# A quarter of one weight load cut into 88 and 40 rows, and four unread matmuls taken out, in a one-token decoder block

## The chip, the cores and the metric

The kernel runs on one core of a Trainium2 chip. Its time is the device time of one execution in microseconds (us), as the median of several runs. The profile is of one execution, recorded by the hardware profiler; its span reaches from the first to the last instruction of the program. PE is TensorE, PEld its weight loads, DVE is VectorE, ACT ScalarE, POOL GpSimd, and SP is SyncE, which here only issues loads and the one store.

## The reference

A decoder block for one new token of two sequences: layer norm, attention over a cache of 8,192 keys and values with 16 heads, a residual, a second layer norm, and a gated feed-forward part without a nonlinearity, with its residual.

```python
B, Sq, D = 2, 1, 448            # H, Sk, Dh = 16, 8192, 256;  F = 1792
q = (layernorm(x) @ wq).reshape(B, Sq, H, Dh).transpose(0, 2, 1, 3)
p = softmax(einsum("bhqd,bhkd->bhqk", q, k_cache) * Dh ** -0.5)
h = x + einsum("bhqk,bhkd->bhqd", p, v_cache).reshape(B, Sq, H * Dh) @ wo
g, u = layernorm(h) @ w_gate, layernorm(h) @ w_up
out = h + (g * u) @ w_down
```

All is float32. Each cache has 2 x 16 x 8,192 x 256 elements, 268 MB.

## The kernel before

**The turns.** There are 32 turns, one for each head of each sequence. For a turn SP loads the keys (128 rows of 64 x 256 elements, 8.4 MB) into one of two buffers, `k0` and `k1`, and the values, of the same size, into `v`. VectorE multiplies the keys by the query and sums each product (lines 436 and 445), TensorE and ScalarE make the exponentials, and TensorE sums the weighted values (line 527) in bank 0.

**The order of the loads.** SP issues all of them itself, in an order written out in lines 261 to 292, and they all go into one queue. A load waits until its buffer is free: keys for the maximum `m` of the turn two before, values for the end `M` of the sums of the turn before. Behind the last keys come `wo` into the free half of the key buffers, the last values in two pieces (48 and 16 of 64 columns), then `wg`, the gate weights, once the last keys are used, then `wu`, the up weights, in three loads, then, once the last values are used, `wd`, the down weights, in six loads. Each of the three up loads and six down loads has a semaphore of its own, so that a matmul can start when its own piece has landed. A load's semaphore counts 16 when all of it is there.

**The last stage**, after the 32 turns. TensorE multiplies the last head by `wo`; ScalarE takes the sum `h`; the norm's centred input is made as `xr` (line 676). Then `project` (line 710) runs twice: the gate, 12 matmuls by line 715 and two by line 726, from `wg`; and up, the same from `wu`. In up, the first 8 of line 715 wait for the first up load (contraction chunks 0 and 1), the next 4 for the second, and the two of line 726 for the third. ScalarE scales the gate (line 746), VectorE multiplies it by up (line 755), TensorE transposes the product (line 760), VectorE copies it (line 767), and TensorE multiplies it by the 14 pieces of `wd`: 8 of them by line 779, the others by line 805, each waiting for its wd load. VectorE copies the result (line 815), and SP stores it.

**Unread matmuls.** `busy(n)` (line 534) issues four matmuls of n columns into bank 4, which nobody reads any more. It is called at six places: before the last turn's transposes (384 columns), twice around `last_head` (256 and 320), between gate and up (384), after up (256) and before the down matmuls (192). They are the L539 of the profile.

**Layout of the up weights.** `wu` lies in memory as 128 rows of 6,272 elements. The first up load takes the first 2 F = 3,584 elements of each row, the second the next F = 1,792, the third the last 896.

Of the kernel before, what the change touches and what calls it, by code (L numbers as in the profile page):

```python
# [8 lines left out]
B, D, H, SK, DH, F = 2, 448, 16, 8192, 256, 1792  # L9
EPS = 1e-5  # L10
P = 128
# [13 lines left out]
NF = F // P  # L25
FH = FG[0] // 2
FF = [(n, g) for n in range(4) for g in range(4) if n < FG[g] // P]
DOWN = (4, 4, 2, 2, 1, 1)
NPART, OPEN_AFTER = 8, 9

LAYOUT = (
# [122 lines left out]
def decode_block(nc, x, k_cache, v_cache, wq, wo, wg, wu, wd, out):  # L154
# [6 lines left out]
    def landing(name):  # L161
        return nc.alloc_semaphore(name=name)
# [4 lines left out]
    V, A, G, S, T = (  # L167
        Engine(nc, *engine)
        for engine in (
            (nc.vector, "dve"), (nc.scalar, "act", ("qsel", "qb"), ("q",)), (nc.gpsimd, "pool"),  # L170
            (nc.sync, "sp"), (nc.tensor, "pe", ("qp", "Q0"), ("heads",)),
        )
    )

    def load(line, dst, src, sem, name, *waits, n=16):
        line.do(lambda: line.e.dma_start(dst, src).then_inc(sem, 16), *waits)  # L176
        known[name] = sem, n
# [63 lines left out]
    wu_t = k_flat[1][:, NF * D : 2 * NF * D]  # L241
# [39 lines left out]
        )  # L281
        at += n
    load(S, wg_t, wg, landing("wg"), "wg", ("m", NQ - 1))
    for k, part in enumerate((slice(0, 2 * F), slice(2 * F, 3 * F), slice(3 * F, NF * D))):
        load(S, wu_t[:, part], wu[:, part], landing(f"wu{k}"), ("wu", k))
    at = 0
    for k, n in enumerate(DOWN):
        load(
# [245 lines left out]
    def busy(n):  # L534


        for g in range(0, P, 32):
            T.do(
                lambda g=g: nc.tensor.matmul(  # L539
                    acc_ps[g : g + B, :n], sel, heads[:, :n], start=True, stop=True  # L540
                )
            )
# [130 lines left out]
    for rows, c, to in LAYOUT:  # L673
        k = rows.stop - rows.start
# [35 lines left out]
    def project(ps, w, landed, done, blank, between=None):  # L710

        for c in range(DC - 1):
            for g, n in enumerate(FG):
                T.do(
                    lambda c=c, g=g, n=n: nc.tensor.matmul(
                        ps[32 * g : 32 * g + 32, :n], xr[:, c].rearrange("p b r -> p (b r)"),
                        w[:, c * F + FO[g] : c * F + FO[g] + n], start=(c == 0), stop=False,
                    ),
                    landed(c), "xr", blank,
                )  # L720
            if c == 1 and between is not None:
                between()
        at = (DC - 1) * F
        for k in range(2):
            T.do(
                lambda k=k, n=FG[2 * k], at=at: nc.tensor.matmul(
                    ps[HALF * k : HALF * k + HALF, :n],
                    xr[:, DC - 1 :].rearrange("p c b r -> p (c b r)"), w[:, at : at + n],
                    start=False, stop=True,
                ),  # L730
                landed(DC - 1), done=done if k == 1 else None,
            )
            at += FG[2 * k]
# [11 lines left out]
    A.do(  # L745
        lambda: nc.scalar.activation(g_sb, g_ps, AF.Copy, scale=rv), "g", "rv", done="g_in",
    )
    busy(384)
    project(u_ps, wu_t, lambda c: ("wu", max(c - 1, 0)), "u", "u_blank")
    busy(256)  # L750
    hm_sb, hmT = late(P, FG[0]), late(P, 4, P)
# [23 lines left out]

    down_of = [k for k, n in enumerate(DOWN) for _ in range(n)]
    for k, (j, g) in enumerate(FF[:NPART]):
# [105 lines left out]
```

## Time and profile before

| | us |
|---|---|
| three runs: median (lowest, highest) | 1301.18 (1301.15, 1301.63) |
| the profiled execution | 1300.94 |
| its span | 1299.6 |
| DVE busy | 1132.5 (87%) |
| PE busy | 471.1 (36%) |
| SP's queue on the 16 DMA engines | 99.8% of the span |

The profiled execution is 0.24 us under the median of the runs, and 1.34 us of it lie outside the span. Busy shares are means over the whole span. In windows, the DMA share is the mean over 16 DMA engines, so that one engine at work alone shows as 0.06. A packet is put into the window in which it starts, so a share can pass 1.00.

### The profile page before, as it was taken

The numbers are of one execution on the slowest core, as the hardware profiler recorded it, in microseconds if no ns is written. First come the engines' busy times: TensorE is split into PE (matmuls) and PEld (weight loads), VectorE is DVE, ScalarE is ACT, GpSimd is POOL, SyncE is SP. The second block draws the span as 40 slices with busy tenths as digits, with TensorE's granted clock in tenths as the row PEclk, the third lists the DMA queues.
The fourth block names the chain that finished last, engine by engine and source line by source line (L and its number), as shares of the span: only waits on it lengthen the run. The fifth ranks groups of instructions, "written<-read, shape, count | busy, mean of one in ns | idle before, by whom it ended". The sixth has DMA issues, their size and how long they took to land.

```text
span 1299.6 us, 7381 instructions
## 1 busy us (share of the span) xinstructions
PE 471.1 (36%) x2870; PEld 149.9 (12%) x2870; DVE 1132.5 (87%) x265; ACT 83.5 (6%) x245; POOL 0.8 (0%) x8
## 2 busy tenths in 40 slices
PE   3643214334323433323334322433322343332368
PEld 0111001101001101101101101101100110100113
DVE  1999988889888889888889988889988888988861
ACT  1100000000000000000000000000000000000000
POOL 0000000000000000000000000000000000000000
PEclk9866566666566666556666656666656666655669
DMA  9999999999999999999999999999999999999998
GB/s 412 428 450 422 448 424 444 426 436 436 422 450 422 450 422 448 424 444 426 436 436 422 450 422 450 422 448 424 444 426 436 436 422 450 422 450 422 448 422 365
DMA packets 11382, 561.28 MB, mean 432 GB/s; under 512 B 1394, under 2 KB 1652, under 8 KB 2420
## 3 DMA queue, kind: packets, MB, share of 16 engines
q1 hardware_dynamic: 11376, 561.25, 99.8%
q8 instruction: 2, 0.03, 0.0%
q10 hardware_dynamic: 4, 0.00, 0.0%
HBM read 561.19 MB, written 0.06 MB: 432 GB/s over the span
## 4 chain that ended last, share of the span: by engine, by line
DMA 48%; DVE 41%; issue 8%; PE 2%; SPq 0%; DVEq 0%; ACT 0%
DMA k<-in_A_k_cache_dram 45%; DVE s L445 21%; DVE k L436 19%; DMA v<-in_wq_dram 2%; DMA v<-in_wd_dram 1%; PE bank L376 1%; PE bank L561 1%; PE bank L527 1%; DVE m L458 0%; DVE nm L464 0%; DVE rl L469 0%; SPq L176 0%; PE bank L551 0%; DVEq L149 0%; PE bank L367 0%
## 5 line engine op out<-in xcount | busy, mean ns | idle before, releaser
L436 DVE TENSOR_TENSOR k<-k,qb 128x4096 f32<-128x4096 f32 x64 | 555.3, 8676 | 122.6 <-DMA k<-in_A_k_cache_dram 98.9
L445 DVE TENSOR_REDUCE s<-k 128x16 f32<-128x4096 f32 x64 | 555.2, 8675 | 1.1
L527 PE MATMUL bank<-v,p 128*2 128x512 f32 x2048 | 289.5, 729 | 348.0 <-DMA v<-in_A_v_cache_dram 348.0
L527 PEld LDWEIGHTS bank<-v,p 128*2 128x2 f32 x2048 | 53.2, 96 | 577.2 <-DMA v<-in_A_v_cache_dram 370.7
L597 PE MATMUL bank<-nm,row 1*128 1x1 f32 x64 | 18.6, 357 | 230.9 <-DVE nm L464 230.9
L594 PE MATMUL bank<-ident,m 128*1 128x128 f32 x32 | 11.9, 372 | 179.7 <-DVE m L458 179.7
L502 ACT ACTIVATE o_sb<-bank 128x512 f32<-128x512 f32 x32 | 19.1, 597 | 625.9 <-PE bank L527 625.9
L597 PEld LDWEIGHTS bank<-nm,row 1*128 1x128 f32 x64 | 15.9, 306 | 240.3 <-DVE nm L464 240.3
L619 PE MATMUL bank<-sel,o_sb 128*128 128x1 f32 x256 | 33.7, 253 | 22.6 <-ACT o_sb L502 22.6
L367 PE MATMUL bank<-q_sel,ones 2*128 2x256 f32 x68 | 40.2, 691 | 0.0
L619 PEld LDWEIGHTS bank<-sel,o_sb 128*128 128x128 f32 x256 | 31.0, 191 | 52.3 <-ACT o_sb L502 52.3
L376 PE MATMUL bank<-v,xz 128*2 x64 | 30.5, 639 | 16.3 <-DMA v<-in_wq_dram 16.3
L492 ACT ACTIVATE nb<-bank 128x1 f32<-128x1 f32 x32 | 5.5, 171 | 427.0 <-PE bank L597 427.0
L601 PE MATMUL bank<-lsum,ones 128*128 128x1 f32 x64 | 18.7, 361 | 23.5 <-ACT p L494 23.5
L594 PEld LDWEIGHTS bank<-ident,m 128*1 128x1 f32 x32 | 2.5, 79 | 182.7 <-DVE m L458 182.7
L601 PEld LDWEIGHTS bank<-lsum,ones 128*128 128x128 f32 x64 | 16.0, 309 | 26.2 <-ACT p L494 26.2
L404 ACT ACTIVATE q_sel<-q_all,ident 2x256 f32 (+1 forms) x35 | 17.2, 492 | 0.0
L413 ACT ACTIVATE qb<-bank 128x256 f32<-128x256 f32 x34 | 13.0, 383 | 58.2 <-PE bank L367 58.2
L367 PEld LDWEIGHTS bank<-q_sel,ones 2*128 2x128 f32 x68 | 16.4, 297 | 2.2 <-issue 1.7
L494 ACT ACTIVATE p<-s,nb 128x64 f32<-128x64 f32 x32 | 11.1, 348 | 1.0
L504 ACT ACTIVATE oT<-bank,rl 128x2 f32 x32 | 8.4, 262 | 42.0 <-PE bank L619 42.0
L487 DVE COPY k<-bank 128x448 f32<-128x448 f32 x1 | 0.6, 624 | 11.6 <-PE bank L561 11.6
(89 smaller groups left out, 96.0 us busy)
## 6 DMA issues: line engine op xcount, KB each, us to landing
v<-in_wq_dram SPq DMA_DIRECT2D x1, 7168.0 KB, 19.7
k<-in_wo_dram SPq DMA_DIRECT2D x1, 7168.0 KB, 39.6
k<-in_A_k_cache_dram SPq DMA_DIRECT2D x1, 6144.0 KB, 38.1
v<-in_A_v_cache_dram SPq DMA_DIRECT2D x1, 6144.0 KB, 22.8
k<-in_wg_dram SPq DMA_DIRECT2D x1, 3136.0 KB, 27.8
k<-in_A_k_cache_dram SPq DMA_DIRECT2D x1, 2048.0 KB, 24.1
v<-in_A_v_cache_dram SPq DMA_DIRECT2D x1, 2048.0 KB, 27.3
k<-in_wu_dram SPq DMA_DIRECT2D x1, 1792.0 KB, 31.8
```

Of the source, the lines that this page charges most:

```text
L367: lambda *_: nc.tensor.matmul(qb_ps, ones[:B, :], q_sel, start=True, stop=True),
L376: lambda turn, k=k, c=c, xs=xs, base=base: nc.tensor.matmul(q_ps[k], xz[:, xs, :], wq_t[:, bass.ds(turn * QG + base, QG)], start=(c == 0), ...
L404: return nc.scalar.activation(q_sel, q_sb[:, bass.ds(at, DH)], AF.Copy, scale=ident[:B, b : b + 1])
L413: lambda *_: nc.scalar.activation(qb[i % 2], qb_ps, AF.Copy),
L436: lambda *_: nc.vector.tensor_mul(kt, kt, q[:, None, :].to_broadcast([P, hi - lo, DH])),
L445: lambda *_: nc.vector.tensor_reduce(s[:, lo:hi], kt, axis=AX.X, op=ALU.add),
L502: A.do(lambda *_: nc.scalar.activation(o_sb, o_ps, AF.Copy), ("M", i), done=("osb", i))
L527: lambda *_, t=t, g=g: nc.tensor.matmul(o_ps[g : g + 2, :], p_t[:, 2 * t : 2 * t + 2], v_sb[:, 2 * t : 2 * t + 2, :], start=(t < 4), stop= ...
L594: lambda *_: nc.tensor.transpose(mT_ps, m_t, ident), ("m", i), done=("T", i)
L597: lambda *_: nc.tensor.matmul(nb_ps, row, nm, start=True, stop=True),
L601: lambda *_: nc.tensor.matmul(l_ps, ones, lsum, start=True, stop=True),
L619: lambda *_, c=c, k=k: nc.tensor.matmul(oT_ps[:, c : c + 1], o_sb[:, (2 * k + c) * P : (2 * k + c + 1) * P], sel[:, k : k + 1], start=(k = ...
```

## The change

The first quarter of the first up load, F / 2 = 896 of its 3,584 elements of each row, is loaded on its own, in two loads: rows 0 to 87 and rows 88 to 127. The rest of the first up load, elements 896 to 3,583 of all rows, follows. All three count on the first up load's semaphore, and its readers wait for 48 in place of 16. The second and third up load are as they were. The four unread matmuls between gate and up are gone; nothing they wrote was read.

```diff
+EVEN = 88
...
-    for k, part in enumerate((slice(0, 2 * F), slice(2 * F, 3 * F), slice(3 * F, NF * D))):
-        load(S, wu_t[:, part], wu[:, part], landing(f"wu{k}"), ("wu", k))
+    wu_ends, s_wu = (2 * F, 3 * F, NF * D), [landing(f"wu{k}") for k in range(3)]
+    for rows in (slice(0, EVEN), slice(EVEN, P)):
+        load(S, wu_t[rows, : F // 2], wu[rows, : F // 2], s_wu[0], "wu_even")
+    for k, part in enumerate(map(slice, (F // 2, *wu_ends), wu_ends)):
+        load(S, wu_t[:, part], wu[:, part], s_wu[k], ("wu", k), n=16 * (3 if k == 0 else 1))
...
-    busy(384)
     project(u_ps, wu_t, lambda c: ("wu", max(c - 1, 0)), "u", "u_blank")
```

On SP, the loads from the gate weights on stood like this before (rows x elements of each load; k and v are the buffers, and waits names the semaphores: dve0 is VectorE's, pe0 TensorE's):

```order
L176 DMA k<-in_wg_dram 128x6272 [waits dve0]
L176 DMA k<-in_wu_dram 128x3584
L176 DMA k<-in_wu_dram 128x1792
L176 DMA k<-in_wu_dram 128x896
L176 DMA v<-in_wd_dram 128x1792 [waits pe0]
```

and stand so now (the line of the helper that issues is now 179):

```order
L179 DMA k<-in_wg_dram 128x6272 [waits dve0]
L179 DMA k<-in_wu_dram 88x896
L179 DMA k<-in_wu_dram 40x896
L179 DMA k<-in_wu_dram 128x2688
L179 DMA k<-in_wu_dram 128x1792
L179 DMA k<-in_wu_dram 128x896
L179 DMA v<-in_wd_dram 128x1792 [waits pe0]
```

SP issues two loads more ahead of the wd loads; nothing else changes place on it.

On TensorE, the end of gate and the start of up before (sel and xr are the left operands, wu0 and wu1 the semaphores of the first two up loads):

```order
L726 MATMUL bank<-k,xr 64x512
L726 MATMUL bank<-k,xr 64x384
L539 MATMUL bank<-k,sel 2x384 x4
L715 MATMUL bank<-k,xr 32x512 [waits dve0,wu0]
L715 MATMUL bank<-k,xr 32x512
L715 MATMUL bank<-k,xr 32x384 x2
```

and now:

```order
L732 MATMUL bank<-k,xr 64x512
L732 MATMUL bank<-k,xr 64x384
L721 MATMUL bank<-k,xr 32x512 [waits dve0,wu0]
L721 MATMUL bank<-k,xr 32x512
L721 MATMUL bank<-k,xr 32x384 x2
```

Up follows the gate's last matmul directly; it waits for the same semaphores.

## The prediction

> **What bounds the kernel now.** I read the page first, for shares and queues.
>
> ```profile
> PE 471.1 (36%) x2870; PEld 149.9 (12%) x2870; DVE 1132.5 (87%) x265; ACT 83.5 (6%) x245; POOL 0.8 (0%) x8
> ...
> DMA packets 11382, 561.28 MB, mean 432 GB/s; under 512 B 1394, under 2 KB 1652, under 8 KB 2420
> ...
> q1 hardware_dynamic: 11376, 561.25, 99.8%
> q8 instruction: 2, 0.03, 0.0%
> q10 hardware_dynamic: 4, 0.00, 0.0%
> ```
>
> Queue 1, which is SP's, keeps the 16 DMA engines busy for 99.8% of the span at a mean of 432 GB/s, or 432 / 16 = 27.0 GB/s for each. The two caches and the weights are 561 MB, and the change moves no byte less. VectorE's 87% lies in front of these transfers and isn't touched. So the end of the kernel is set by when the last bytes arrive, and only the last stage can give anything. Its chain of waits, from the issue of the last wd load on:
>
> ```profile
> 1279.27 0.04 issue
> 1279.31 17.89 DMA v<-in_wd_dram
> 1297.20 0.04 issue
> 1297.24 0.44 PE bank L805 x8
> 1297.69 0.02 issue
> 1297.71 0.27 DVE k L815
> ```
>
> The last wd load lands at 1297.20 us; only eight records of matmul, one copy and the store of the result come after it. A finer look is at the same stretch by windows; the columns are the window, its length, busy time (and count) of PE, PEld, DVE, ACT and POOL, the granted clock, the DMA share and GB/s.
>
> ```profile
> 1290.00:1291.00 1.00, 1.00 (x6) 0.20 (x4) 0.00 (x0) 0.00 (x0) 0.00 (x0) 1.00 1.01 423
> 1291.00:1292.00 1.00, 1.00 (x12) 0.31 (x10) 0.74 (x2) 0.00 (x0) 0.00 (x0) 1.00 1.00 419
> 1292.00:1293.00 1.00, 1.00 (x16) 0.48 (x18) 0.78 (x3) 0.00 (x0) 0.00 (x0) 1.00 1.00 409
> 1293.00:1294.00 1.00, 0.77 (x12) 0.07 (x8) 0.00 (x0) 0.00 (x0) 0.00 (x0) 1.00 1.01 412
> 1294.00:1295.00 1.00, 0.86 (x8) 0.04 (x8) 0.07 (x1) 0.00 (x0) 0.00 (x0) 1.00 1.01 396
> 1295.00:1295.60 0.60, 0.45 (x16) 0.38 (x16) 0.56 (x1) 0.00 (x0) 0.00 (x0) 1.00 0.85 326
> 1295.60:1296.00 0.40, 0.40 (x16) 0.16 (x8) 0.00 (x0) 0.00 (x0) 0.00 (x0) 1.00 0.22 81
> 1296.00:1296.90 0.90, 0.76 (x26) 0.51 (x24) 0.00 (x0) 0.00 (x0) 0.00 (x0) 1.00 0.13 48
> 1296.90:1298.80 1.90, 0.58 (x16) 0.16 (x8) 0.27 (x1) 0.00 (x0) 0.00 (x0) 1.00 0.00 0
> ```
>
> The sixteen DMA engines do not stop together. The share falls from 0.85 to 0.22 at about 1295.6 and to 0.13 after 1296.0: 0.22 x 16 = 3.5 engines, then 0.13 x 16 = 2.1. So about thirteen are done by 1295.6, one or two more by 1296.0, and two work on alone to 1296.9, 1.3 us behind the mass. The last landing waits for those two. The likely cause is in the queue rows: two packets of kind "instruction" took DMA time during the run. This is the row of the second, from the DMA view of 1282 to 1284 us:
>
> ```profile
> q8 instruction: 1, 0.02, 3.0%
> ```
>
> 3.0% of 16 engines' 2 us is 0.96 us of one engine. The view of 77 to 79 us shows the other. Each would put one engine behind by about the 1.3 us seen, and with the queue never empty it cannot catch up. That is a reading; no row numbers the engines.
>
> **The change part by part.** The split load first. Where were the up loads issued and when did they land?
>
> ```profile
> L176 SPq DMA_DIRECT2D k<-in_wu_dram x3: 419/433/433, 1254.6 to 1255.6; - x3
> ...
> k<-in_wu_dram SPq DMA_DIRECT2D x1, 1792.0 KB, 31.8
> k<-in_wu_dram SPq DMA_DIRECT2D x1, 896.0 KB, 33.4
> ...
> k<-in_wu_dram SPq DMA_DIRECT2D x1, 448.0 KB, 34.0
> ```
>
> *Issue.* Two more issues on SP at 0.43 us each are 0.87 us. Behind them on SP stand the six wd loads and the store. SP's next wait ends at 1276.97 (row below), the three issues end at 1255.6 + 0.4 = 1256.0, so 21 us of idle SP hide it, and the transfers themselves start some 25 us after their issue in any case. Cost 0; uncovered it would be 0.87 us.
>
> *Bytes.* The quarter is 128 rows of 3,584 B, 0.459 MB: 1.06 us at 432 GB/s, or 1.11 at the 412 GB/s of the window from 1293, where packets of this size run. Smaller packets thus cost at most 0.05 us on all engines.
>
> *Which engine moves what.* By count, SP issues 79 loads and stores of 128 rows each (4 ahead of the loop, 61 in it, 14 behind), and 79 x (128 + 16) = 11,376, exactly queue 1's packets: one packet for each row and one closing packet for each of 16 engines. The only short transfer is x:
>
> ```profile
> x<-in_A_x_dram ACTq DMA_DIRECT2D x1, 3.5 KB
> ```
>
> Its 2 rows gave queue 10's four packets, 2 + 2: two engines. Both fit a rule of equal shares, 8 rows on each of 16 engines and 1 row on each of 2. By equal shares 88 rows go to 11 engines (8 each) and 40 to 10 (4 each), the greatest divisors up to 16. If both start at the same end of the list, ten engines carry 12 rows of the quarter in place of 8, one carries 8, five none. A row takes 3,584 B / 27.0 GB/s = 0.133 us, so the ten finish 0.53 us later and the five 1.06 us earlier. The bounds from rows: if instead rows are spread as evenly as they go (5 or 6 and 2 or 3 to an engine), nothing moves by more than one row, 0.13 us.
>
> [...] No run here has yet shown which engines a load of 88 rows uses.
>
> *What that does to the end.* Before, the mass ends at 1295.6, the one or two between at 1296.0 and the two late ones at 1296.9.
>
> - Case A, both late engines among the five: they end at 1296.9 - 1.06 = 1295.84. The mass goes to 1295.6 + 0.53 = 1296.13, the one between to 1296.53 if it is among the ten. The last is then at 1296.13 to 1296.53: 0.37 to 0.77 us earlier. I take 0.37, since the engine between has 11 chances in 16 to be outside the five, and with it the packets' 0.05 us: -0.32 us.
> - Case B, one of the two among the ten: it ends at 1296.9 + 0.53 + 0.05, so +0.58 us.
>
> Even a perfect levelling, with the surplus of the late ones dealt out to all, gains no more than 1.3 - 2.1 x 1.3 / 16 = 1.1 us.
>
> *The removed matmuls.* From the timeline, with start, duration and engine:
>
> ```profile
> 1276.97 3.27 SPq L176 DMA_DIRECT2D v<-in_wd_dram  x6
> ...
> 1286.82 0.83 PE L539 MATMUL bank<-k,sel 128*2 128x384 f32 x8
> ...
> 1287.46 2.74 PE L715 MATMUL bank<-k,xr 128*32 128x512 f32 x24
> ...
> 1290.14 1.07 PE L726 MATMUL bank<-k,xr 128*64 128x512 f32 x4
> ...
> 1292.77 0.94 PE L779 MATMUL bank<-v,k 128*2 128x448 f32 x8
> 1293.93 0.11 PEld L779 LDWEIGHTS bank<-v,k 128*2 128x2 f32 x8 [1.05 <-DMA v<-in_wd_dram]
> 1293.93 0.93 PE L779 MATMUL bank<-v,k 128*2 128x448 f32 x8 [0.23 <-DMA v<-in_wd_dram]
> ...
> 1297.24 0.40 PE L805 MATMUL bank<-v,k 128*32 128x112 f32 x8 [0.16 <-DMA v<-in_wd_dram]
> ```
>
> Without L539 up can start at 1286.82 in place of 1287.46, 0.64 us earlier; its first load landed at 1254.63 + 31.8 = 1286.4. Its L726 then waits for the third up load, 1255.6 + 34.0 = 1289.6, in place of starting at 1290.14: about 0.5 us gained on PE. But PE then only waits longer for wd: at 1293.93 the second wd load holds it already, and it is the last wd load that holds it at 1297.24. So this edit gives 0 by itself. In case A it gives slack to a PE that would have only the 0.23 and 0.16 us of these two waits left; if PE's work were late, up to 0.2 us of A would be lost.
>
> *The wait on the first up load* now counts three transfers. It lands as a whole at 1286.4, or 0.53 later (1286.9) in the worst case, against PE's arrival at 1286.82: at most 0.1 us, which the 0.5 us freed covers.
>
> *The PE clock.* The removed work kept PE without a pause. What does a pause do? Two rows, of a pause before the last turn and of the end:
>
> ```profile
> 1249.00:1254.20 5.20, 0.00 (x0) 0.00 (x0) 5.17 (x2) 0.22 (x1) 0.00 (x0) 0.76 1.14 495
> ...
> 1295.00:1299.60 4.60, 2.19 (x56) 1.20 (x56) 0.83 (x2) 0.00 (x0) 0.00 (x0) 0.99 0.20 71
> ```
>
> In 5.2 us of idle the mean clock is 0.76, so it was full for 0.52 of it, 2.7 us, and half after. At the end, with PE busy for 2.19 of 4.6 us, it stayed at 0.99. The new pause is 0.5 us: cost 0. [...]
>
> **The sum.** The profiled execution took 1300.94 us, 1.34 over its span of 1299.6, and 0.24 under the median of three, 1301.18. Case A gives 1300.94 - 0.32 = 1300.62, that is 1300.86 against the median.
>
> **The rivals.** *B, one late engine carries more* (+0.58): 1301.76. For it: five places in sixteen are few, and drawn blindly both late engines are in them only in one case of twelve. Against it: an engine that fetches code need not be drawn at random, and two late engines need not be far apart. No row settles it, so choosing A over B is a judgment.
>
> *E, the change does not do what it says*: rows are spread evenly, or the engine of 8 rows is the late one. 0 to +0.05: 1301.2. For it: no row shows a load of 88 rows, so an even spread is not excluded. Against it: the equal shares in the counts of packets. [...]
>
> *C, the clock halves*, the side slower by more than 0.2%. If the pauses in up or ahead of wd reach some 2.7 us, PE's remaining groups (from L726 to L805, 6.8 us busy from 1290 on by the windows above) run at half the clock. The 3.8 us of them from 1293 on would take 3.8 us longer, all of them 6.8. Less the waits for wd that this swallows, about 1 us, it is 2.8 to 5.8: 1304.0 to 1307.0. Against it: the pause is a fifth of what the clock bore.
>
> **How the numbers follow.** About 0.2%, 2.6 us, is what a measurement of this kernel can tell from no change. A has 0.50, B 0.33, E 0.14, C 0.03. A, B and E all lie within 2.6 us; no mechanism above gains over 1.1, which leaves 0.01 for faster, and C gives 0.03 for slower. The forecast is A's 1300.9, no change that can be told. The range reaches from A's best, 0.77 us less (1300.4), to B's 1301.8 with 0.2 us for the runs' own spread: 1300.4 to 1302.0. C is left out.
>
> **What would show it.** Right: in the windows of the last 3 us, the share stays above 0.5 to about 1296.1 and then drops within 0.5 us; the last wd landing at 1296.9 or before; L726 of up starting at about 1289.6; the clock at 1.00. B: a thin tail of 0.06 to 0.13 for 2 us and more, the last landing near 1297.8. E: the windows as before. Wrong altogether: a clock of 0.5 before 1297, or a span that differs by over 2.6 us.

## The result, and the profile after

The changed kernel takes 1302.96 us (median of 22 runs, 1301.87 to 1305.43), against 1301.18 for the kernel before (22 runs, 1300.96 to 1301.73): a ratio of 1.0016, with a 95% interval of 1.001 to 1.0021. That is 1.8 us slower, less than the 0.2% (2.6 us) that the prediction took as the least that can be told, and yet clear: the fastest run of the changed kernel is slower than the slowest of the kernel before. It lies outside the predicted range of 1300.4 to 1302.0. One thing about the median has to be known: the 22 runs of the changed kernel lie in two groups, 12 of them from 1301.87 to 1303.11 (median 1302.09) and 10 from 1304.00 to 1305.43 (median 1304.61), with nothing between, while those of the kernel before lie in one group of 0.8 us. So there are two amounts to explain, 0.9 us that every run loses, and 2.5 us more in nearly half of them.

The profiled execution of the changed kernel took 1303.11 us, the highest of the lower group; its span is 1301.8. The queues on its page:

```profile
DMA packets 11531, 561.28 MB, mean 431 GB/s; under 512 B 1415, under 2 KB 1673, under 8 KB 2569
...
q1 hardware_dynamic: 11525, 561.25, 99.8%
q8 instruction: 2, 0.03, 0.0%
```

The bytes are the same, and queue 1 has 11,525 - 11,376 = 149 packets more: 128 rows and 21 closing packets. 21 is 11 + 10, so the 88 rows went to 11 engines and the 40 to 10, as the equal shares said.

The windows of the kernel before, in the microseconds in which the short loads will run (columns as in the prediction; the last two are DMA share and GB/s):

```profile
1281.00:1282.00 1.00, 1.00 (x11) 0.90 (x11) 0.02 (x1) 0.00 (x0) 0.00 (x0) 1.00 1.00 430
1282.00:1283.00 1.00, 1.00 (x8) 0.36 (x10) 0.89 (x6) 0.00 (x0) 0.00 (x0) 1.00 1.00 418
1283.00:1284.00 1.00, 1.00 (x15) 0.47 (x8) 0.68 (x4) 0.00 (x0) 0.00 (x0) 1.00 0.97 401
1284.00:1285.00 1.00, 1.00 (x12) 0.46 (x10) 0.06 (x1) 0.00 (x0) 0.00 (x0) 1.00 0.92 387
```

The same of the changed kernel, then its end:

```profile
1281.00:1282.00 1.00, 0.96 (x9) 0.58 (x7) 0.17 (x1) 0.35 (x2) 0.00 (x0) 1.00 1.05 297
1282.00:1283.00 1.00, 1.00 (x10) 0.69 (x10) 0.41 (x3) 0.00 (x0) 0.00 (x0) 1.00 1.06 233
1283.00:1284.00 1.00, 0.39 (x3) 0.00 (x0) 0.83 (x6) 0.00 (x0) 0.00 (x0) 1.00 1.07 215
1284.00:1285.00 1.00, 0.75 (x10) 0.43 (x14) 0.35 (x2) 0.00 (x0) 0.00 (x0) 1.00 0.96 317
1285.00:1286.00 1.00, 1.00 (x12) 0.17 (x4) 0.00 (x0) 0.00 (x0) 0.00 (x0) 1.00 1.08 437
...
1297.00:1297.60 0.60, 0.36 (x17) 0.34 (x16) 0.48 (x1) 0.00 (x0) 0.00 (x0) 1.00 0.86 329
1297.60:1298.20 0.60, 0.60 (x20) 0.20 (x11) 0.14 (x1) 0.00 (x0) 0.00 (x0) 1.00 0.60 227
1298.20:1299.10 0.90, 0.81 (x24) 0.51 (x24) 0.00 (x0) 0.00 (x0) 0.00 (x0) 1.00 0.06 22
```

From 1281 to 1285 the sixteen engines are as busy as ever, at shares of 0.96 to 1.07, and yet move 215 to 317 GB/s in place of 387 to 430. The share says here that packets were under way, not that they went at full rate: in the packet records of this trace a row of 3,584 bytes takes 140 ns elsewhere in this stage, and 259 ns in the median of those that start in the microsecond from 1282. At the end the shape that case A forecast is there, though 2 us late. The mean share is 0.60 until 1298.2, and then 0.06, one engine of sixteen, is alone for 0.9 us; before, two engines were alone, 1.3 us behind. In another execution of the changed kernel, after_look1 below, no engine is left alone for long:

```profile
1297.80:1298.40 0.60, 0.60 (x24) 0.23 (x12) 0.00 (x0) 0.00 (x0) 0.00 (x0) 1.00 0.20 75
1298.40:1299.00 0.60, 0.43 (x12) 0.16 (x8) 0.00 (x0) 0.00 (x0) 0.00 (x0) 1.00 0.00 0
```

The same stage of the changed kernel's profile in the timeline:

```profile
1255.23 2.08 SPq L179 DMA_DIRECT2D k<-in_wu_dram  x5
...
1284.25 1.91 PE L721 MATMUL bank<-k,xr 128*32 128x512 f32 x16 [0.86 <-DMA k<-in_wg_dram]
...
1288.64 1.91 PE L721 MATMUL bank<-k,xr 128*32 128x512 f32 x16 [0.18 <-DMA k<-in_wu_dram]
...
1290.78 1.05 PE L721 MATMUL bank<-k,xr 128*32 128x512 f32 x8 [0.23 <-DMA k<-in_wu_dram]
...
1291.85 1.07 PE L732 MATMUL bank<-k,xr 128*64 128x512 f32 x4
...
1296.12 0.93 PE L784 MATMUL bank<-v,k 128*2 128x448 f32 x8 [0.70 <-DMA v<-in_wd_dram]
...
1299.39 0.40 PE L810 MATMUL bank<-v,k 128*32 128x112 f32 x8 [0.16 <-DMA v<-in_wd_dram]
```

From the gate weights on, PE waits for a transfer ahead of nearly every group that reads a new load; before, its matmuls waited for none of this stage's loads until the wait for wd at 1293.93 (row in the prediction). The last matmuls start at 1299.39 in place of 1297.24, 2.15 us later. Of these, 0.6 us were there ahead of the short loads: the up loads are issued from 1255.23 on, in place of 1254.6. That is part of what makes this execution the slowest of its group. The other 1.5 us come in from the short loads on.

### The profile page after: what moved, and what is told of

It reads as the page before. It is cut to its first block, busy times and chain, and to the rows that moved or that the text cites. A ratio compares the mean times of both kernels' runs of the same rounds, so it can differ in the third digit from the quotient of the medians.

```text
span 1301.8 us, 7367 instructions
## 1 busy us (share of the span) xinstructions
PE 469.5 (36%) x2862; PEld 149.4 (11%) x2862; DVE 1132.6 (87%) x265; ACT 83.5 (6%) x245; POOL 0.8 (0%) x8
## 3 DMA queue, kind: packets, MB, share of 16 engines
q1 hardware_dynamic: 11525, 561.25, 99.8%
## 4 chain that ended last, share of the span: by engine, by line
DMA 75%; PE 25%; issue 0%; SPq 0%; DVE 0%
DMA v<-in_A_v_cache_dram 72%; PE bank L533 22%; PE bank L382 2%; DMA v<-in_wq_dram 2%; DMA v<-in_wd_dram 1%; SPq L179 0%; PE bank L373 0%; PE bank L810 0%; DVE k L820 0%
## 5 line engine op out<-in xcount | busy, mean ns | idle before, releaser
L508 ACT ACTIVATE o_sb<-bank 128x512 f32<-128x512 f32 x32 | 19.1, 597 | 628.0 <-PE bank L533 628.0
```

What stands on the lines that cost most here:

```text
L508: A.do(lambda *_: nc.scalar.activation(o_sb, o_ps, AF.Copy), ("M", i), done=("osb", i))
```

## The experiments

Theories of the 0.9 us: **T1**, rows that lie next to each other in a short load are contested: they hold one another up, by something that no view names, and so take about twice as long (259 ns in place of 140 in the profile after); the dip of the windows is theirs. **T2**, the shares of 11 and 10 engines are unequal, and an engine that had no slack has more to carry. **T2b**, short loads cost as such. **T3**, it is the removed matmuls. **T4**, it is smaller packets. Theories of the second group: **T5**, the clock halves; **T6**, a transfer comes later. Each kernel below starts from the kernel before; every time stands against the kernel before on the same chip.

**split_only, nobusy_only: the two parts of the change apart.** The first has the change's loads and keeps all unread matmuls; the second only leaves out the four:

```diff
-    busy(384)
     project(u_ps, wu_t, lambda c: ("wu", max(c - 1, 0)), "u", "u_blank")
```

> The kernel before with the split of the quarter into 88 and 40 rows alone; the four unread matmuls stay. [...] Theory 2 (unequal shares alone, a late engine given 12 rows for 8): +0.6 us and no dip. Theory 3 (the removed matmuls cost it, by a pause of PE): within 0.2 us of before.

> The kernel before without the four unread matmuls between gate and up; loads as before. Theories 1 and 2: within 0.2 us of before, since PE waits for the down weights at 1293.9 and 1297.2 us anyway. Theory 3: +1.3 to +2.5 us.

split_only: 1302.28 us (11 runs) against 1301.16, ratio 1.0015 [1.0005, 1.0024], with 4 of its 11 runs at 1304.42 to 1304.9. nobusy_only: 1301.53, 1.0002 [0.9993, 1.0011], in one group. That is 0.37 us above before, over the 0.2 that was expected, but inside the interval, and its runs (1300.97 to 1301.87) overlap with those of before (1300.82 to 1301.84). The split alone has both the loss and the second group. T3, which expected 1.3 us or more, falls; a few tenths are not excluded.

**halves64: equal shares, contested rows** (shown against split_only's loads, with EVEN = 88, as is the next).

```diff
-    for rows in (slice(0, EVEN), slice(EVEN, P)):
+    for rows in (slice(0, 64), slice(64, P)):
```

> The kernel before with the quarter as rows 0 to 63 and rows 64 to 127; the unread matmuls stay. Both loads give 4 rows to each of 16 engines, so shares are equal. [...] Theory 2: within 0.2 us of before, no dip.

**cols_only: the quarter as a load of its own, all 128 rows.**

```diff
-    for rows in (slice(0, EVEN), slice(EVEN, P)):
-        load(S, wu_t[rows, : F // 2], wu[rows, : F // 2], s_wu[0], "wu_even")
+    load(S, wu_t[:, : F // 2], wu[:, : F // 2], s_wu[0], "wu_even")
```

> The kernel before with the quarter (896 elements of each row) as a load of its own over all 128 rows; the unread matmuls stay. Theories 1 and 2: within 0.2 us of before (one issue more and smaller packets, 0.05 us). Theory 4 (smaller packets or one load more are what costs): +1 us or more.

halves64: 1302.98 (1302.55 to 1303.33), 1.0013 [1.0004, 1.0022], 1.8 us more, and one group. cols_only: 1301.25 (1301.13 to 1301.7), 1.0 [0.9991, 1.0009]. The windows of the same microseconds, of cols_only:

```profile
1281.00:1282.00 1.00, 1.00 (x11) 0.94 (x12) 0.00 (x0) 0.00 (x0) 0.00 (x0) 1.00 1.08 448
1282.00:1283.00 1.00, 1.00 (x8) 0.36 (x10) 0.88 (x6) 0.00 (x0) 0.00 (x0) 1.00 1.04 441
1283.00:1284.00 1.00, 1.00 (x15) 0.47 (x8) 0.71 (x4) 0.00 (x0) 0.00 (x0) 1.00 0.99 414
1284.00:1285.00 1.00, 1.00 (x12) 0.43 (x10) 0.03 (x1) 0.00 (x0) 0.00 (x0) 1.00 0.96 391
```

and of halves64, with its last microseconds:

```profile
1281.00:1282.00 1.00, 1.00 (x11) 0.93 (x12) 0.00 (x0) 0.00 (x0) 0.00 (x0) 1.00 1.35 294
1282.00:1283.00 1.00, 0.81 (x4) 0.17 (x2) 0.88 (x6) 0.00 (x0) 0.00 (x0) 1.00 0.68 204
...
1296.60:1297.20 0.60, 0.37 (x12) 0.17 (x12) 0.30 (x1) 0.00 (x0) 0.00 (x0) 1.00 0.41 155
1297.20:1297.80 0.60, 0.60 (x24) 0.36 (x18) 0.32 (x1) 0.00 (x0) 0.00 (x0) 1.00 0.12 48
1297.80:1298.40 0.60, 0.53 (x24) 0.35 (x16) 0.00 (x0) 0.00 (x0) 0.00 (x0) 1.00 0.10 39
1298.40:1299.00 0.60, 0.58 (x20) 0.16 (x8) 0.00 (x0) 0.00 (x0) 0.00 (x0) 1.00 0.05 18
```

The same bytes in the same small packets go at 441 GB/s when all 128 rows are in one load, and at 204 when two halves follow each other. T4 falls, and T2 can't be the cause of the dip: by the equal shares every engine carries 8 rows here, as before, and the loss is larger than in split_only's lower runs (1.1 us). It is larger than the 0.8 to 1.3 us of the author's estimate for T1 (0.46 MB at half the rate are 1.06 us more). The end shows where. By the equal shares no engine is spared, and the two late ones (shares of 0.12 and 0.10) still run alone, and one of them (0.05) goes on behind that. By the packet records most engines end at about 1296.8 here and at 1295.6 before, which is 1.2 us as T1 has it; but the last packet of wd ends at 1298.84 and 1296.90, so the last engine is 2.0 us behind the others in place of 1.3. Why it falls back further is not shown.

**extra_step4, extra_next: short loads beside the old ones.** The up loads stay whole. Eight loads of 8 rows, 0.23 MB that nobody reads, go into spare room ahead of them, with rows four apart or neighbouring; equal shares and sizes in both (each kernel has one of the two marked lines; in both, SP waits for these loads before it clears the semaphores at the end):

```diff
+    spare, s_extra = k_flat[1][:, NJ * DH - F :], landing("extra")
+    for cols in (slice(0, F // 2), slice(F // 2, F)):
+        for at in range(4):
+            rows = slice(at, 32, 4)              # extra_step4
+            rows = slice(8 * at, 8 * at + 8)     # extra_next
+            load(S, spare[rows, cols], wu[rows, cols], s_extra, "extra", n=16 * 8)
```

> The kernel before with eight loads more between the gate and the up loads, each of 8 rows of 896 elements into spare room that nobody reads: rows 0, 4, ... 28, then 1, 5, ... 29, and so on, twice. 0.23 MB more, 8 rows of 3,584 B more on each of eight engines, 1.07 us of their time. [...] Theory 2b (short loads cost as such, whichever rows they write): the same as extra_next.

> As extra_step4, but each of the eight loads writes 8 rows that lie next to each other: 0 to 7, 8 to 15, 16 to 23, 24 to 31, twice. Same bytes, same engines, same number of loads and packets. [...] Theory 2b: within 0.3 us of extra_step4.

extra_step4: 1301.31 against 1301.30, 1.0001 [0.9992, 1.001]. extra_next: 1302.28, 1.001 [1.0001, 1.0019], with 5 of 11 runs at 1303.2 to 1304.04 and six at 1301.4 to 1302.28 (median 1301.83). One of the 11 runs of extra_step4 lies at 1302.73, the others at 1301.0 to 1301.8. Windows of extra_step4, then of extra_next:

```profile
1281.00:1282.00 1.00, 1.00 (x11) 0.84 (x11) 0.09 (x1) 0.00 (x0) 0.00 (x0) 1.00 1.05 437
1282.00:1283.00 1.00, 1.00 (x10) 0.38 (x12) 0.89 (x6) 0.00 (x0) 0.00 (x0) 1.00 1.03 432
```

```profile
1281.00:1282.00 1.00, 1.00 (x11) 0.92 (x12) 0.00 (x1) 0.00 (x0) 0.00 (x0) 1.00 1.21 312
1282.00:1283.00 1.00, 0.84 (x8) 0.20 (x6) 0.89 (x6) 0.00 (x0) 0.00 (x0) 1.00 0.69 251
```

This is the cleanest pair: eight short loads each, of the same size, and only which rows lie in one load differs. Four apart there is no dip and no loss in the median; side by side there is the dip, which costs 0.5 us in the lower group, and the second group, with which the median is 0.97 us above four apart. T1's direction holds, at less than the 1.5 us or more between the two that the author had estimated. T2b falls.

**split_double: twice the contested bytes.** Both short loads have F columns in place of F / 2.

> split_only with twice the columns in the two short loads (F = 1,792 elements of each row, half of the first up load); the unread matmuls stay. [...] Theory 2 (shares alone): ten engines are 1.07 us later than in an even split, no dip, +0.3 to +0.6 us.

1304.85 (5 runs) against 1301.15, 1.0035 [1.0021, 1.0049]; its lower three runs are 3.7 us above before (median 1304.82), where split_only's seven are 1.1 (1302.24); the other two lie at 1306.83 and 1307.32. Windows:

```profile
1281.00:1282.00 1.00, 0.97 (x10) 0.94 (x10) 0.17 (x1) 0.00 (x0) 0.00 (x0) 1.00 1.12 262
...
1286.00:1287.00 1.00, 1.00 (x10) 0.20 (x4) 0.22 (x2) 0.00 (x0) 0.00 (x0) 1.00 1.11 151
...
1288.00:1290.00 2.00, 0.60 (x8) 0.00 (x0) 0.00 (x0) 0.58 (x1) 0.00 (x0) 1.00 0.97 403
```

The dip now lasts to 1288, at 262 to 136 GB/s. It grows with the contested bytes, as T1 has it, but by more than twice; the author's estimate was twice split_only's loss, 1.8 to 2.6.

**The second group: split_warm, and four single executions.** split_warm is split_only with eight unread matmuls more ahead of the gate, to keep the clock up (`busy(448)` twice before `project` of the gate). warm_look1 and warm_look2 are single executions of it, after_look1 and after_look2 of the changed kernel, to catch an execution of each group.

> split_only with eight unread matmuls of 448 columns more in front of the gate, where PE waits for the late gate load and in one profile fell to half its clock. Theory 5 (the runs of the split kernels above 1304 us are those in which the clock halves in the last stage): no run above 1303.5 us, and a clock of 1.00 from 1281 us to the end. Theory 6 (these runs have another cause, in the transfers): some 4 of 11 runs above 1304 us as in split_only.

> The changed kernel once more, for a second profile of it: its runs fall into two groups, near 1302.0 and near 1304.5 us. Theory 5: a run near 1304.5 shows a clock of 0.50 in some windows after 1283 us, a run near 1302.0 does not. Theory 6: both show 1.00 there, and the slower one differs in its landings.

> split_warm once more for a profile in its slower group of runs (7 of 11 lay near 1304.7 us). Theory 5 (clock): a run near 1304.7 shows windows of 0.50 after 1283 us. Theory 6 (transfers): it shows 1.00, and an engine's landings lie some 2.5 us behind those of a run near 1302.0. A run near 1302.0 tells nothing.

> As warm_look1, a third execution of the same kernel with a profile.

> The changed kernel for a third profile. Near 1304.5 us: theory 5 expects a clock of 0.50 in windows after 1283 us, theory 6 a clock of 1.00 and one engine's landings some 2.5 us later than at 1302 us.

split_warm: 1304.69 (1301.86 to 1305.3), 1.0021 [1.0012, 1.003], with 7 of 11 runs at 1304.67 and above; T5 expected the second group to go. warm_look1 (1301.88) fell into the lower group and warm_look2 (1302.69) near its top (in both, later packets of 7,168 bytes take the usual 272 ns); they tell nothing of the other. after_look1 took 1302.34 us, after_look2 1304.59: one of each group, and the only profile of the upper one. Of after_look1, ten microseconds behind the dip:

```profile
1286.00:1296.00 10.00, 8.92 (x76) 2.05 (x68) 1.68 (x5) 0.69 (x1) 0.00 (x0) 1.00 1.00 417
```

Of after_look2, the same:

```profile
1286.00:1296.00 10.00, 8.20 (x68) 1.90 (x60) 1.54 (x5) 0.69 (x1) 0.00 (x0) 1.00 1.00 349
```

And queue 1 in the DMA views of 1292 to 1294 us (packets, MB, share), of after_look1:

```profile
q1 hardware_dynamic: 137, 0.81, 96.7%
```

and of after_look2:

```profile
q1 hardware_dynamic: 110, 0.69, 98.8%
```

The clock is 1.00 in both: T5 falls. Both have much the same dip. Behind it, one returns to 417 GB/s, and the other goes on at 349, at a full share. By the DMA rows a megabyte takes 0.967 x 32 / 0.81 = 38.2 us of one engine in the first and 0.988 x 32 / 0.69 = 45.8 in the second, 1.20 times as much. The packet records show it in every size: 7,168 bytes take 272 ns in one and 328 in the other, 3,584 bytes 140 and 159 to 169, 1,792 bytes 74 and 86, the closing packets 9 and up to 13. It ends at about 1299.0: three engines run out of packets at about 1298.8, and from 1299 on 1,792 bytes take 74 ns (median) there too, while thirteen engines still work. From 1285 to 1299, 14 us x (1 - 349 / 417) = 2.3 us; the two executions differ by 2.25. So T6 holds for this execution in that transfers make the second group, but not as it had it, with one engine behind: all of them are slower.

**early_split, split96: how long, and with which loads?** early_split leaves the up loads whole and cuts the first keys instead, ahead of the 32 turns; split96 is split_only with 96 and 32 rows, of which every engine has 6 and 2.

```diff
-    load(S, k_sb[0][:, :HC], keys_of(k_cache, 0, 0, HC), landing("k0"), "k0")
+    s_k0 = landing("k0")
+    for rows in (slice(0, 88), slice(88, P)):
+        load(S, k_sb[0][rows, :4], keys_of(k_cache, 0, 0, 4)[rows], s_k0, "k0_cut")
+    load(S, k_sb[0][:, 4:HC], keys_of(k_cache, 0, 4, HC), s_k0, "k0", n=16 * 3)
```

> The up load whole and the unread matmuls kept, as before; instead the first keys, ahead of the 32 turns, are loaded in three pieces: their first 4 of 64 columns (4,096 bytes of each row) in two loads of 88 and 40 rows, then the rest. Theory S (after the contested rows the queue falls into a slower rhythm that lasts as long as it is never empty): some 4 to 6 of 11 runs at a rate of about 345 in place of 430 GB/s for much of the 1,280 us that follow, tens to 200 us longer; the others within 2 us of before. Theory Z (the slow rhythm ends by itself within some tens of us, or belongs to the small rows of the weights): all runs within 4 us of before. The dip itself by either: rows of 4,096 bytes at about twice their time, 1 to 2 us lost in the profile's first 40 us.

> The unread matmuls kept; the quarter of the first up load cut into 96 and 32 rows in place of 88 and 40, so that both loads divide into 16 equal shares (6 and 2 rows of each engine) and no engine is spared. Contested rows (T1): the dip as in the 88/40 cut, 215 to 300 GB/s for some 4 us, and the lower runs 1 to 2 us above before. Theory K (the slower group of times comes from loads that leave some engines out): one group of runs, within 1 us, as with halves of 64 rows. Theory U (it comes with any contested pair of unequal loads): again 4 to 6 of 11 runs some 2.5 us above the others.

early_split: 1302.82 (10 runs) against 1301.51, 1.0011 [1.0002, 1.0021]; five runs at 1302.13 to 1302.3 and five at 1303.35 to 1303.6. split96: 1302.66 (1302.21 to 1303.1, 10 runs), 1.001 [1.0, 1.002], one group. Windows of early_split, whose profile is of its lower group:

```profile
19.00:21.00 2.00, 0.27 (x1) 0.09 (x2) 0.00 (x0) 0.00 (x0) 0.00 (x0) 1.00 0.93 262
21.00:23.00 2.00, 2.00 (x3) 0.25 (x2) 0.00 (x0) 0.00 (x0) 0.00 (x0) 1.00 1.22 227
```

The dip is where the short loads are, also 1,260 us earlier. The lower group is 0.7 us above before, less than the 1 to 2 that were expected. The groups are 1.3 us apart (medians 1302.24 and 1303.52), not tens or hundreds: theory S falls, Z holds. If the upper group is the same rhythm of 1.2, it lasted some 1.3 / (1 - 1 / 1.2) = 8 us (an estimate) and then ended; no profile of it shows how. split96 has a shorter dip than expected, 330, 211 and 378 GB/s in the three microseconds from 1281, and bears out K: with contested loads that by the equal shares leave no engine out, halves64 and split96, none of 21 runs is in a second group; with 88 and 40 or with 8 rows, neighbouring, a third to two thirds are. Leaving engines out is not enough for it: the loads of extra_step4 leave eight out as well.

## Why the prediction was wrong, point by point

- *Issue*: right. The up loads' issue takes 2.08 us in place of three by 0.43, some 20 us ahead of SP's next wait, and the last wd load still lands 19.1 us after its issue (17.9 before), behind a full queue.
- *Bytes*, smaller packets at most 0.05 us: right in size, by cols_only, 0.09 us above before in the median.
- *Which engine moves what*, equal shares on 11 and 10 engines: right, by the 149 packets.
- *Case A*, the late engines among the five that are spared: right in its shape. One engine is alone at the end, or none for long, where there were two, and against halves64, where none is spared and the thin tail remains, split_only's lower runs (1302.24) are 0.7 us faster. That difference is the levelling only as far as the two dips cost alike, which no run separates. (One slip that changes nothing: only the ten would hold back the engine between, so the smaller gain had 10 chances in 16, not 11. That both loads start at the same end of the list, which the 12, 8 and no rows rest on, no view shows: none numbers the engines.)
- *The removed matmuls*, 0 by themselves: not contradicted by nobusy_only, whose 0.37 us are inside its interval. *The wait on the first up load* and *the clock*: no cost was seen; the clock of the changed kernel's profile is 1.00. But the premise that PE's clock bears a pause of some 2.7 us did not hold in split_only's profile (last section).
- **The step that failed**: "A row takes 3,584 B / 27.0 GB/s = 0.133 us, so the ten finish 0.53 us later and the five 1.06 us earlier." The rate was that of loads of 128 rows, and the step took it to belong to the engine alone, whatever rows it writes and whoever writes beside it. The runs showed 259 ns in place of 140 for such a row, and a slower rate for the other packets beside them too: in the changed kernel 10,752 bytes took 775 ns (median of those from 1282 to 1283), in cols_only 404. Against cols_only, whose windows from 1281 to 1285 show 448, 441, 414 and 391 GB/s, the changed kernel moved 448 + 441 + 414 + 391 - 297 - 233 - 215 - 317 = 632 KB less in the four microseconds, which is 1.5 us at 430 GB/s (after_look1, nearer the middle of the group, moved 624 KB less). Less case A's gain of 0.37 this gives an estimate of +1.1; the lower group's median is +0.9.
- **What was no rival at all**: a slower rate for every engine. Each rival dealt the rows to engines in another way, or changed PE's clock; none let the same engine move fewer bytes in the same busy time. Of the 1.8 us that the median moved, 0.9 are the dip's; the rest is there because ten of 22 runs in the second group put the median at the top of the lower one. That the forecast missed its range by 1 us and not by 0.1 is owed to this group, which no rival had foreseen.

That rows of one load contend by which rows they are is shown by extra_step4 against extra_next: eight rows four apart cost nothing in the median, at 437 and 432 GB/s in the two microseconds from 1281, and eight neighbours cost 0.5 us in the lower group, at 312 and 251; halves of 64 rows go at 294 and 204 there. By what they contend is not shown: the rows lie four apart or side by side in SBUF, the on-chip memory that holds the buffers, and in memory as well, no run moves one without the other, and no view names what they would share. For rows spread evenly the prediction's rival E counted 0 to 0.05 us; halves64, with equal shares, measured 1.8 us for 0.46 MB.

**Open**: why, behind a dip made by loads that leave engines out, every packet goes on taking 1.2 times as long in about half of the executions, and what ends it. It is not the clock of PE and not one late engine. In after_look2 it ended when three engines had run out of packets; in early_split, where the queue goes on for another 1,260 us, its 1.3 us can't have lasted until the end, so that is not the only way in which it ends. That it is a rhythm between the engines which loads on all sixteen don't set off is a guess that fits split96 and halves64. Whether it is the rows' places in SBUF or in memory is open, as said. A cut with rows four apart, which by extra_step4 might deal fewer rows to the late engines without the dip, was not tried, so whether the levelling alone would beat the kernel before is open too.

## What to carry to other kernels

In this saturated stream the loads that kept the full rate were those over all 128 rows (441 GB/s in cols_only from 1282 to 1283), and short ones with rows four apart (432 in extra_step4). Loads of some neighbouring rows, levelled by engines or not, slowed all the engines: in the changed kernel by a fifth to a half for four microseconds (297, 233, 215 and 317 GB/s in place of 430, 418, 401 and 387), for 0.46 MB. If a short load must be, try rows four apart rather than neighbours (tested here with loads of eight rows alone), and measure it with runs enough to see a second group. Read a DMA share and the GB/s beside it together: a share of 1.0 with a falling rate at the same packet sizes meant here that each packet took longer, which a sum over engines at a fixed rate cannot show.

## What the runs showed of the hardware

- By the packet records of the kernel before, from 1255 us on, packets of one size took one time, to the nanosecond: all 384 of 3,584 bytes 140 ns, all 384 of 7,168 bytes 272, all 128 of 25,088 bytes 931, and 126 of 128 of 14,336 bytes 535. So a single packet that something held up stands out: the one of 14,336 bytes at 1,001 ns starts at 1283.90, where the second instruction packet, of 961 ns from 1282.95, ends (the other took 541).
- In split_only's profile the granted clock fell to 0.50 behind a pause of only some 0.8 us on PE (0.79 in the row below), shorter than the 2.7 us that the prediction worked out. The same pause is in the changed kernel (0.86, row above), at a clock of 1.00 throughout. The timeline and the windows of split_only:

```profile
1283.63 3.47 PE L718 MATMUL bank<-k,xr 128*32 128x512 f32 x16 [0.79 <-DVE k L702]
...
1298.02 0.95 PE L808 MATMUL bank<-v,k 128*32 128x112 f32 x32
1299.04 0.27 DVE L818 COPY k<-bank 128x112 f32<-128x112 f32 x1 [1.29 <-PE bank L808]
```

```profile
1283.00:1284.00 1.00, 0.36 (x4) 0.16 (x8) 0.71 (x4) 0.00 (x0) 0.00 (x0) 0.92 0.74 197
1284.00:1285.00 1.00, 1.00 (x10) 0.57 (x6) 0.00 (x0) 0.00 (x0) 0.00 (x0) 0.50 0.94 382
...
1287.00:1288.00 1.00, 1.00 (x12) 0.55 (x10) 0.32 (x2) 0.00 (x0) 0.00 (x0) 0.87 1.03 434
```

By the windows from 1283 to 1288 it was at half for 0.16 + 3 + 0.26 = 3.4 us, and the 16 records of matmul took 3.47 us in place of the 1.91 of the changed kernel's. That execution took 1302.28 us, the median of split_only. It was not free: behind it PE waits for no wd load any more, since its own work ends last. The last wd load landed 18.9 us after its issue at 1279.3, at about 1298.2; the last copy, which in the kernel before starts 0.5 us behind that landing (1297.20 and 1297.71), starts at 1299.04. So the half clock cost some 0.3 us here, by estimate. What decides whether such a pause halves the clock, no run here tells.
